# A fused attention and gated feed-forward kernel: the first tokens loaded in four tiles, all weights on one queue, the first ratios sent through DRAM

## Chip, cores and metric

The kernel runs on one core of one Trainium2 chip. The time is the device time of one execution in microseconds (us), and the median of several executions is quoted. Before the change it was 271.02 us (three executions, 270.77 to 271.33). Executions are sorted by state; only fast ones are compared.

Engines in the profile: PE is TensorE (matmul), PEld its weight loads, DVE VectorE, ACT ScalarE, POOL GpSimd, SP SyncE. A row such as `SPq` or `ACTq` is the issue of a transfer by that engine. The row of a stretch has its length, then busy time of PE, PEld, DVE, ACT, POOL, clock, DMA share, GB/s.

## The reference, cut to what matters

```python
# x: 2048 tokens x 512, bf16; 32 heads of 16; 4 segments of 512 tokens; feed-forward 1792 wide
def _A_ref(x, wq, wk, wv, wo, beta):          # attention within a segment, plus a memory of earlier ones
    g = _sigmoid(beta).reshape(1, H, 1, 1)
    for s in range(N):
        logits = q_s @ k_s^T * scale + causal mask
        a_dot = softmax(logits) @ v_s
        a_mem = (phi(q_s) @ M) / (phi(q_s) @ z + 1e-06)      # the "recall"
        o = g * a_mem + (1.0 - g) * a_dot
        M, z = M + phi(k_s)^T @ v_s, z + sum(phi(k_s))
    return o @ wo
def _B_ref(x, W_gate, W_up, W_down):
    return ((x @ W_gate) * relu-mask * (x @ W_up)) @ W_down
g = _sigmoid((x * gate_w).sum(-1, keepdims=True))            # one gate for each token
return g * _A_ref(...) + (1 - g) * _B_ref(...)
```

(The products are abridged; the shapes and the order are the reference's.)

## The kernel before

The kernel gives each instruction as a task with a cost and a priority to a small planner; the planner's simulation fixes the order on each engine, and a table of small shifts (`SHIFT`) tunes that order. Three parts matter here.

The loads at the start. Two engines issue transfers, SyncE (`nc.sync`) and ScalarE (`nc.scalar`):

```python
    def load_halves(dst, src, k, name):
        src = src.rearrange("(c p) n -> p c n", p=P)
        nc.sync.dma_start(out=dst[:, 0:k // 2], in_=src[:, 0:k // 2])
        nc.scalar.dma_start(out=dst[:, k // 2:k], in_=src[:, k // 2:k])
        return [arrival(name + h) for h in "ab"]
    # ...
    got_n[0] = load_halves(xn, x[0:L, :], 4, "n")        # the first 512 tokens, two halves
    got_q = load_halves(wq_sb, A_wq, NC, "q")
    got_k = load_cols(nc.sync, wk_sb, A_wk, 0, D, "k")
    got_v = load_cols(nc.scalar, wv_sb, A_wv, 0, D, "v")
    nc.scalar.dma_start(out=betab[:], in_=A_beta.partition_broadcast(P))   # 64 bytes to each partition
    load_gu(0)
```

The start of TensorE: seven junk matmuls, sixteen transposes of the loaded tokens, then the first projection with wq:

```python
        for k in range(7):
            nc.tensor.matmul(bank(warm[k % 8]), lhsT=junk[:, 0:P], rhs=junk[:], start=True,
                             stop=True)
    # ...
        pairs = [(c, t) for h in range(2) for c in range(2) for t in (2 * h, 2 * h + 1)]
        pairs += [(c, t) for c in (2, 3) for t in range(4)]      # chunk c, token tile t
```

The ratios of the token gates. `rcol` holds them by token; the attention needs them spread over partitions. In the first segment a small matmul spreads them, later ones go through DRAM:

```python
        if seg == 0:
            # ... q0 = rcol * quad on VectorE
            d = plan.add("PE", 260, key, lambda: nc.tensor.matmul(
                bank(sl)[:, 0:16], lhsT=fold.rearrange("p j q -> p (j q)"),
                rhs=q0.rearrange("p b t -> p (b t)"), start=True, stop=True), [d], PEL, need=[sl])
        else:
            a = plan.add("SP", 360, key, lambda: nc.sync.dma_start(
                out=ratio[seg].rearrange("q b t -> b q t"), in_=rcol[:, seg, 0:4]), [c], 2800)
            d = plan.add("SP", 360, key, lambda: nc.sync.dma_start(
                out=rq[seg % 2][:], in_=ratio[seg].rearrange("q b t -> q (b t)")[None]
                .to_broadcast([4, 32, 16])), [a, att.get(("gate", seg - 2))], 2300)
```

The scaled gates `grc` are then one VectorE product, and every attention output of the segment needs them. The recalls of later segments need coefficients `cdr`, which go out to DRAM and come back by two further transfers.

The softmax here doesn't subtract the row's maximum and nothing guards it: scores larger than these inputs give would overflow.

Of the kernel before, what the change touches and what calls it, by code (L numbers as in the profile page):

```python
# [12 lines left out]
P = 128  # L13
# [19 lines left out]
    34: 106376, 36: 113032, 40: -114448, 53: 61670, 57: 13693, 68: 19011, 76: -24569, 79: 9811,  # L33
    83: 74173, 96: 13617, 110: 46210, 203: 58110, 206: -52557, 224: -57564, 227: 1792,
    230: -40586, 233: 13336, 239: 4861, 242: 18866, 245: 1040, 248: -5909, 251: 9703, 254: 598,
    257: 3431, 263: 6249, 265: 184723, 266: 16148, 269: 14619, 272: 3105, 275: 1832, 281: 4406,
    284: 3910, 287: 8594, 289: 93691, 290: -97554, 302: -129776, 339: 46969, 340: 26203,
    351: -125117, 352: -49927, 357: -75265, 365: 12721, 369: 106054, 370: -69909, 374: -148035,
    376: -85788, 378: 3424, 382: 76139, 383: -116528, 389: 34360, 391: 49594, 395: 81165,
    396: 6755, 398: -114708, 404: 5060, 407: -180212, 410: -53419, 413: -3953, 426: 67665,  # L40
    486: 79762, 487: 34701, 549: 20214, 552: 20622, 558: -10377, 561: -19405, 564: 39907,
    570: -12896, 573: 9701, 576: -9651, 582: -16069, 585: 22538, 588: 33613, 591: -4380,
    594: -4590, 603: 3888, 606: 7821, 609: 4156, 612: 8910, 615: -8330, 618: 8398, 624: 10060,
    630: 14623, 633: 38130, 657: -107064, 669: 31434, 682: 109150, 684: -73474, 685: -119916,
    688: 38815, 703: 145579, 705: -95722, 708: 12868, 713: 6919, 726: 31160, 730: 132280,
    734: -54441, 739: -10455, 747: -49618, 752: 229700, 753: -104580, 755: -97169, 761: -147428,
    821: 62605, 851: 29329, 862: -95255, 892: 8128, 895: 66022, 898: 3515, 901: 3081, 904: 8787,
    910: -7899, 913: -6480, 916: -5672, 922: -5022, 928: -20540, 931: -12044, 934: 2538,
    937: 18155, 939: 121046, 940: -2598, 943: 4141, 949: 20268, 955: 16548, 958: -12595,
    964: -16200, 966: -94268, 967: 6793, 973: 22963, 976: 20987, 988: 376830, 1039: 13799,  # L50
    1044: 2818, 1049: -146392, 1054: -57834, 1059: 9401, 1069: -10731, 1071: 101628,
    1074: -107652, 1082: -19522, 1085: 14735, 1088: 14474, 1099: 70503, 1101: 119386,
    1132: -110039, 1161: -106277, 1162: 240923, 1192: -69003, 1212: 109678, 1213: 112279,
    1221: 8139, 1224: 31863, 1227: 14005, 1230: 100895, 1233: 19137, 1236: 79863, 1239: -20537,
    1242: -16128, 1245: -20639, 1248: 150158, 1251: -735, 1254: 26992, 1260: 49993, 1263: 17068,
    1269: 7685, 1272: -7301, 1278: 76110, 1281: 68111, 1284: 44327, 1287: -37198, 1290: 24997,
    1296: -21740, 1299: -12793, 1302: 89596, 1305: -52927, 1329: 147560, 1341: -68166,
    1353: 29837,
# [157 lines left out]
def kernel(  # L216
# [73 lines left out]
    def work():  # L290
# [3 lines left out]
    LANDS = dict(na=4300, nb=4600, qa=5650, qb=6050, k=9300, v=9750, g0=11800, u0=13300, gw=13900, g1=15200, u1=16700,  # L294
                 x1=18400, g2=20400, u2=21600, g3=22800, u3=24000, d0=27700, d1=30400, o=31800, x2=33600)

    def arrival(name):
        return plan.add("in_" + name, 0.0, 0.0, None, lat=LANDS[name])
# [7 lines left out]

    def load_halves(dst, src, k, name):
        src = src.rearrange("(c p) n -> p c n", p=P)
        nc.sync.dma_start(out=dst[:, 0:k // 2], in_=src[:, 0:k // 2])
        nc.scalar.dma_start(out=dst[:, k // 2:k], in_=src[:, k // 2:k])  # L310
        return [arrival(name + h) for h in "ab"]
# [19 lines left out]
    got_n[0] = load_halves(xn, x[0:L, :], 4, "n")  # L331
    got_q = load_halves(wq_sb, A_wq, NC, "q")
    got_k = load_cols(nc.sync, wk_sb, A_wk, 0, D, "k")
    got_v = load_cols(nc.scalar, wv_sb, A_wv, 0, D, "v")
# [6 lines left out]
    got_x[1] = [arrival("x1")] * NC  # L341
    junk = sb([P, L], BF16, "junk")
    nc.vector.memset(junk[:], 0.0)
# [5 lines left out]
    got_x[2] = [arrival("x2")] * NC  # L349
# [20 lines left out]
    for i in range(2):  # L370
        nc.gpsimd.memset(Vp[i][:, :, :, DH:18], 1.0)
        nc.gpsimd.memset(zbd[i][:], 0.0)

    fold = sb([P, 4, 32], F32, "fold")
    nc.vector.tensor_reduce(out=fold[:, 0], in_=ident.rearrange("p (b q) -> p q b", b=4),
                            op=ALU.add, axis=mybir.AxisListType.X)
    nc.vector.tensor_copy(fold[:, 1:4], fold[:, 0:1].to_broadcast([P, 3, 32]))
    quad = sb([P, 4], F32, "quad")
    nc.vector.memset(quad[:], 0.0)
    for b in range(4):  # L380
        nc.vector.memset(quad[32 * b:32 * b + 32, b:b + 1], 1.0)
# [44 lines left out]
    def gate_tasks(seg):  # L426
# [17 lines left out]

        if seg == 0:
            sl, q0 = work(), sb([P, 4, 4], F32, "q0")
            d = plan.add("DVE", 90, key, lambda: nc.vector.tensor_tensor(
                q0[:], rcol[:, seg, None, 0:4].to_broadcast([P, 4, 4]),
                quad[:, :, None].to_broadcast([P, 4, 4]), ALU.mult), [c], DVL, lock=True)
            d = plan.add("PE", 260, key, lambda: nc.tensor.matmul(  # L450
# [457 lines left out]
```

## Time and profile before

| | before |
|---|---|
| median (range), 6 executions beside the changed kernel | 271.17 us (270.70 to 271.76) |
| span of the profiled execution | 270.2 us |
| TensorE busy | 265.3 us, 98% |
| first transpose, first wq matmul | 4.29, 5.97 us |
| first score group | 12.58 us |

A score group is one set of query times key matmuls whose results ScalarE exponentiates in a single 1.88 us instruction. There are 80.

The prediction shows most lines. Two more views are needed. First the DMA rates in the first 12 us, in 40 slices of 0.3 us:

```profile
GB/s 0 0 0 0 0 0 27 79 290 352 375 372 383 382 382 382 379 318 276 348 372 324 307 331 365 379 365 365 379 333 216 122 76 119 208 316 389 386 382 386
```

The rate stays above 270 from 2.4 to 9.0 us. It falls to 76 at about 9.6 us; those are the slices in which beta's small packets run, behind wv on ScalarE's queue. By then wq and wk are in place. Second, the stretch in which the second segment's recalls begin (length, then busy time of PE, PEld, DVE, ACT, POOL, clock, DMA share, GB/s):

```profile
78.00:104.00 26.00, 26.00 (x226) 10.46 (x225) 19.69 (x45) 19.33 (x16) 9.84 (x16) 1.00 0.16 47
```

TensorE is busy in all 26.00 of 26.00 us.

### The profile page before, as it was taken

The numbers are of one execution on the slowest core, as the hardware profiler recorded it, in microseconds if no ns is written. First come the engines' busy times: TensorE is split into PE (matmuls) and PEld (weight loads), VectorE is DVE, ScalarE is ACT, GpSimd is POOL, SyncE is SP. The second block draws the span as 40 slices with busy tenths as digits, with TensorE's granted clock in tenths as the row PEclk, the third lists the DMA queues.
The fourth block names the chain that finished last, engine by engine and source line by source line (L and its number), as shares of the span: only waits on it lengthen the run. The fifth ranks groups of instructions, "written<-read, shape, count | busy, mean of one in ns | idle before, by whom it ended". The sixth has DMA issues, their size and how long they took to land.

```text
span 270.2 us, 5601 instructions
## 1 busy us (share of the span) xinstructions
PE 265.3 (98%) x2247; PEld 112.2 (42%) x2247; DVE 194.8 (72%) x423; ACT 195.5 (72%) x175; POOL 83.6 (31%) x142
## 2 busy tenths in 40 slices
PE   8999999999999999999999999999999999999995
PEld 4443434444443443444443434344344334444543
DVE  4788999999889667999986776689773736285223
ACT  2299899989897768899877896789888678413100
POOL 3013343333343333333324333243333342300000
PEclk9999999999999999999999999999999999999999
DMA  7999991313431103201210021001100120000002
GB/s 231 316 267 347 242 157 21 97 19 79 105 97 31 32 21 120 22 0 22 85 42 22 1 77 35 19 2 58 29 2 0 33 97 22 19 0 2 0 10 68
DMA packets 29841, 19.25 MB, mean 71 GB/s; under 512 B 14840, under 2 KB 28280, under 8 KB 29816
## 3 DMA queue, kind: packets, MB, share of 16 engines
q1 hardware_dynamic: 28600, 17.84, 25.3%
q10 hardware_dynamic: 1216, 1.06, 1.2%
q8 instruction: 17, 0.28, 0.5%
q14 instruction: 8, 0.07, 0.1%
HBM read 13.21 MB, written 2.55 MB: 58 GB/s over the span
## 4 chain that ended last, share of the span: by engine, by line
PE 90%; DMA 3%; DVE 2%; ACT 2%; issue 1%; POOL 0%; SPq 0%; DVEq 0%; ACTq 0%
PE ps L485 71%; PE ps L606 9%; PE ps L648 6%; DMA cdr<-coefs 2%; ACT E L626 2%; PE ps L841 1%; DMA coefs<-dnr 1%; PE ps L735 1%; PE ps L502 1%; PE ps L754 1%; DVE hT L805 0%; POOL E L635 0%; DVE T L680 0%; DVE dnr L719 0%; DVE omr L740 0%
## 5 line engine op out<-in xcount | busy, mean ns | idle before, releaser
L626 ACT ACTIVATE E<-ps 128x2048 bf16<-128x2048 f32 x80 | 150.4, 1880 | 32.0 <-PE ps L606 23.3
L635 POOL TENSOR_SCALAR_AFFINE_SELECT E<-E 128x512 bf16<-128x512 bf16 x128 | 81.4, 654 | 150.4 <-ACT E L626 150.4
L485 PE MATMUL ps<-xT,wg_sb 128*128 128x512 bf16 x224 | 57.8, 380 | 0.0
L485 PE MATMUL ps<-xT,wu_sb 128*128 128x512 bf16 x224 | 56.7, 380 | 0.5 <-DVE omr L740 0.5
L805 DVE TENSOR_TENSOR hT<-ps,rgr 128x512 bf16<-128x512 f32 x56 | 37.7, 685 | 25.7 <-ACT rgr L799 13.6
L485 PE MATMUL ps<-wd_sb,hT 128*128 128x512 bf16 (+1 forms) x238 | 54.9, 367 | 0.0
L799 ACT ACTIVATE rgr<-ps 128x512 bf16<-128x512 f32 x56 | 32.6, 599 | 20.1 <-PE ps L485 19.8
L485 PEld LDWEIGHTS <-hT 128*128 128x128 bf16 x238 | 22.0, 98 | 25.2 <-issue 3.7
L485 PEld LDWEIGHTS <-wu_sb 128*128 128x128 bf16 x224 | 20.4, 98 | 26.5 <-issue 5.0
L485 PEld LDWEIGHTS <-wg_sb 128*128 128x128 bf16 x224 | 20.3, 98 | 25.9 <-issue 4.1
L827 DVE TENSOR_SCALAR osr<-ps,ngcol 128x512 bf16<-128x512 f32 (+1 forms) x17 | 12.0, 708 | 16.9 <-PE ps L485 16.8
L680 DVE STREAM_TRANSPOSE T<-ps 128x512 f32<-128x512 f32 x32 | 20.8, 685 | 3.1 <-PE ps L648 3.0
L648 PE MATMUL ps<-E,Vp 128*17 128x256 bf16 (+3 forms) x512 | 21.3, 300 | 0.0
L485 PE MATMUL ps<-xT,wk_sb 128*128 128x512 bf16 x64 | 17.4, 379 | 0.0
L606 PE MATMUL ps<-QT,KTe 32*128 32x512 bf16 (+3 forms) x256 | 17.3, 302 | 0.0
L606 PE MATMUL ps<-QT,KTo 32*128 32x512 bf16 (+3 forms) x256 | 17.1, 299 | 0.1
L485 PE MATMUL ps<-xT,wq_sb 128*128 128x512 bf16 x64 | 17.1, 389 | 0.0
L485 PE MATMUL ps<-wo_sb,oT 128*128 128x512 bf16 (+1 forms) x68 | 17.0, 367 | 0.0
L485 PE MATMUL ps<-wv_sb,xT 128*128 128x512 bf16 x64 | 16.8, 380 | 0.0
L648 PEld LDWEIGHTS <-Vp 128*17 128x17 bf16 x512 | 10.9, 91 | 12.4 <-issue 3.8
L606 PEld LDWEIGHTS <-KTe 32*128 32x128 bf16 x256 | 5.1, 91 | 20.3 <-issue 19.9
L740 DVE TENSOR_TENSOR omr<-ps,cdr 128x512 bf16<-128x512 f32 x12 | 8.1, 686 | 7.3 <-DMA cdr<-coefs 6.9
(80 smaller groups left out, 207.9 us busy)
## 6 DMA issues: line engine op xcount, KB each, us to landing
cdr<-coefs SPq DMA_DIRECT2D x12, 256.0 KB
out_dram<-osr SPq DMA_DIRECT2D x15, 128.0 KB
wd_sb<-in_B_W_down_dram SPq DMA_DIRECT2D x2, 896.0 KB
xn<-in_A_x_dram SPq DMA_DIRECT2D x3, 512.0 KB
wg_sb<-in_B_W_gate_dram SPq DMA_DIRECT2D x2, 512.0 KB
wu_sb<-in_B_W_up_dram SPq DMA_DIRECT2D x2, 512.0 KB
wg_sb<-in_B_W_gate_dram SPq DMA_DIRECT2D x2, 384.0 KB
wu_sb<-in_B_W_up_dram SPq DMA_DIRECT2D x2, 384.0 KB
```

The costliest lines, as they stand in the source:

```text
L485: nc.tensor.matmul(bank(sl)[:, 0:width], lhsT=lhsT, rhs=rhs, start=(start and q == 0), stop=(stop and q == n - 1))
L502: nc.tensor.transpose(bank(sl[c]).bitcast(BF16)[:, t * P:(t + 1) * P], xn[:, t, c * P:(c + 1) * P], ident[:])
L606: nc.tensor.matmul(ps[:, j * L + off:j * L + off + n], lhsT=kt[32 * j:32 * j + 32, kb * P:(kb + 1) * P], rhs=QT[i][32 * j:32 * j + 32, kb ...
L626: nc.scalar.activation(Ef[:, e0 * L:e1 * L], ps[:, e0 * L:e1 * L], ACT.Exp, scale=SCALE),
L635: nc.gpsimd.affine_select(out=m, in_=m, compare_op=ALU.is_ge, fill=0.0, base=0, pattern=[[0, 4], [1, P]], channel_multiplier=-1)
L648: nc.tensor.matmul(bank(sl)[32 * j:32 * j + HW, kb * P:kb * P + w], lhsT=Vp[i][:, kb, 8 * c + 2 * j + r, 0:HW], rhs=E[(NFILL * u + f) % RE ...
L680: done.append(plan.add("DVE", 633, key - RL, lambda r=r, sl=sl: nc.vector.transpose(T[ts.i][:, r], bank(sl)), [a] + done, 75 if r else 0, ...
L735: a = plan.add("PE", 216, key, lambda: nc.tensor.matmul(bank(sl), lhsT=mbd[i][:, c].rearrange("p j r e -> p (j r e)"), rhs=pqT[u % RQ][:], ...
L740: a = plan.add("DVE", 605, key - RL, lambda: nc.vector.tensor_tensor(omr[om.i][:], bank(sl), cdr[cs.i][:], ALU.mult), [a, b], DVL, need=[o ...
L799: r = plan.add("ACT", 478, key - RL, lambda sl=gsl, rs=rs: nc.scalar.activation(rgr[rs.i][:], bank(sl), ACT.Relu), [g], ACL, frees=[gsl])
L805: nc.vector.tensor_tensor(hT[hs1.i][:], bank(sl), rgr[rs.i][:], ALU.mult)),
L827: b = plan.add("DVE", 95 + 1.12 * w, key - RL, lambda: nc.vector.tensor_scalar(osr[os.i][:, 0:w], bank(sl)[:, 0:w], ngcol[:, tt:tt + 1], N ...
```

## The change

The intent is a shorter start and a little less TensorE work: x arrives in four tiles on two queues and each is transposed when it lands; all weights follow in order on one queue; one warm-up matmul fewer; the ratio matmul goes. The order of everything was fitted again.

```diff
 SHIFT = {                                     # a wholly new table; cut
-    got_n[0] = load_halves(xn, x[0:L, :], 4, "n")
-    got_q = load_halves(wq_sb, A_wq, NC, "q")
+    got_n[0] = [load(nc.scalar if t % 2 else nc.sync, xn[:, t, :], x[t * P:(t + 1) * P, :],
+                     "n%d" % t) for t in range(4)]
+    got_q = [load_cols(nc.sync, wq_sb, A_wq, 256 * i, 256 * i + 256, "q" + "ab"[i])
+             for i in range(2)]
     got_k = load_cols(nc.sync, wk_sb, A_wk, 0, D, "k")
-    got_v = load_cols(nc.scalar, wv_sb, A_wv, 0, D, "v")
+    got_v = load_cols(nc.sync, wv_sb, A_wv, 0, D, "v")
     nc.scalar.dma_start(out=betab[:], in_=A_beta.partition_broadcast(P))
 # cut
-    nc.vector.memset(junk[:], 0.0)
+    nc.vector.memset(junk[:, 0:P], 0.0)
 # cut: fold and quad, the constants of the ratio matmul, go
-        if seg == 0:
-            # cut: the ratio matmul
+        eng, que, cost = ("SP", nc.sync, 360) if seg else ("ACT", nc.scalar, 520)
+        a = plan.add(eng, cost, key, lambda: que.dma_start(
+            out=ratio[seg].rearrange("q b t -> b q t"), in_=rcol[:, seg, 0:4]), [c], 2800)
+        d = plan.add(eng, cost, key, lambda: que.dma_start(
+            out=rq[seg % 2][:], in_=ratio[seg].rearrange("q b t -> q (b t)")[None]
+            .to_broadcast([4, 32, 16])), [a, att.get(("gate", seg - 2))], 2300)
 # cut: transposes and copies of x by token tile, in five parts, the last tile's in two
+        parts = [(0, 0, 4), (1, 0, 4), (2, 0, 4), (3, 0, 2), (3, 2, 4)]
-        for k in range(7):
-            nc.tensor.matmul(bank(warm[k % 8]), lhsT=junk[:, 0:P], rhs=junk[:], start=True,
+        for k in range(6):
+            nc.tensor.matmul(bank(warm[k % 8]), lhsT=junk[:, 0:P],
+                             rhs=junk[:, None, 0:P].to_broadcast([P, 4, P]), start=True,
                              stop=True)
```

## The prediction

> **What bounds the kernel now.** I read the page's header first, then busy time by stretch, then the start of the kernel in order of time, then the waits, and last the two places that those views pointed at.
>
> From the page:
>
> ```profile
> PE 265.3 (98%) x2247; PEld 112.2 (42%) x2247; DVE 194.8 (72%) x423; ACT 195.5 (72%) x175; POOL 83.6 (31%) x142
> PE 90%; DMA 3%; DVE 2%; ACT 2%; issue 1%; POOL 0%; SPq 0%; DVEq 0%; ACTq 0%
> ```
>
> TensorE is the bound: 98% busy, and 90% of the chain that ended last. Busy is not full speed, so I checked the spacing of starts. In this piece, ten full matmuls take from 29.91 to 32.16, 2.25 us: ten times 0.216 and about 0.1 for going from full-array matmuls to the four-row-group ones of L606.
>
> ```profile
> 29.91 1.02 PE L485 MATMUL ps<-xT,wk_sb 128*128 128x512 bf16 x4
> 30.77 1.46 PE L485 MATMUL ps<-xT,wg_sb 128*128 128x512 bf16 x6
> 32.16 0.40 PE L606 MATMUL ps<-QT,KTe 32*128 32x384 bf16 x8
> ...
> 22.42 0.29 PE L450 MATMUL ps<-q,fold 128*128 128x16 f32 x2
> 22.56 0.59 PE L485 MATMUL ps<-xT,wu_sb 128*128 128x512 bf16 x2
> ```
>
> So in the steady part TensorE has nothing to gain except work taken away. The last two lines show one such piece: the first segment's ratio matmul takes 22.42 to 22.56, 0.14 us.
>
> The start, where the change acts:
>
> ```profile
> 0.80 0.46 SPq L309 DMA_DIRECT2D xn<-in_A_x_dram  x1
> 1.25 3.17 PE L841 MATMUL ps<-junk 128*128 128x512 bf16 x7 [1.25 <-DVE mcol_e L359]
> 4.29 1.62 PEld L502 LDWEIGHTS <-xn 128*128 128x128 bf16 x16 [0.78 <-DMA xn<-in_A_x_dram]
> 4.29 1.89 PE L502 MATMUL ps<-ident,xn 128*128 128x128 bf16 x16
> 5.15 0.43 DVE L519 COPY xT<-ps 128x512 bf16<-128x512 bf16 x1 [2.37 <-PE ps L502]
> 5.97 4.08 PE L485 MATMUL ps<-xT,wq_sb 128*128 128x512 bf16 x16
> 6.83 2.73 PEld L485 LDWEIGHTS <-wq_sb 128*128 128x128 bf16 x13 [0.28 <-issue]
> ```
>
> Seven warm-up matmuls (0.43 us each) fill 1.25 to about 4.24; x lands at 4.29; sixteen transposes at 0.105 us run without a gap to 5.97, where the first projection begins. Its first matmuls are still 0.43 us apart (5.97, 6.40, 6.83); the sixteen together end at 9.89, so thirteen take 3.06 and the fast rate begins just after 6.83.
>
> Waits of TensorE and of VectorE on a transfer:
>
> ```profile
> DVE omr L740 <- DMA cdr<-coefs: 6.9, 4, 4.1
> PE ps L485 <- DVE omr L740: 0.5, 1, 0.5
> ...
> 191.14 1.03 PE L485 MATMUL ps<-wv_sb,xT 128*128 128x512 bf16 x4
> 192.62 0.59 PE L485 MATMUL ps<-xT,wu_sb 128*128 128x512 bf16 x2 [0.45 <-DVE omr L740]
> ```
>
> The only real stall after the start is this one: four matmuls from 191.14 should end at 192.00, and the next starts at 192.62, so 0.62 us are lost. Two PSUM banks were held by the memory read-out (recall) while its coefficients came back through DRAM.
>
> **What the Trainium skill says.** "TensorE: Matmul & The Clock Gate", What's actually happening: the clock starts at half speed and is released after a busy window of about 3.4 us; the window is free-running, so the moment varies. The trace agrees in size: starts 0.43 apart until 6.83, then 0.216, so release came 5.6 us after the first warm-up matmul, between one and two windows. Same page, Back-to-back issue gap: N/2.4 + 2.5 ns, 216 ns for 512 columns; the trace has 0.216. "DMA: Bandwidth & Descriptors", Issuing engines are not separate DMA queues: a second issuing engine saves only issue time, which here is 0.46 us a transfer. "Trainium Kernel Development and Optimization", Performance Expectations, says that matmul busy time is a bad measure of the distance to the roofline; the 0.62 us stall below 98% busy agrees, and it is why I count starts and not the 98%.
>
> **The change part by part.**
>
> 1. *Warm-up.* Six matmuls for seven, on a tile whose memset is a quarter as wide (64 columns of 32 bits against 256, 0.27 us now). I take 0.16 off the memset: start at 1.09. Six at 0.43, the first a little shorter as now, end at about 3.63.
>
> 2. *x in four tiles.* Now two 256 KB halves, issued at 0.80 on two queues, the first landing at 4.29. A tile is half of that; at the 335 to 347 GB/s that the busy stretches of the start move, 128 KB less on a shared stream is about 0.4 us earlier on one queue, and 0.7 at best. So the first tile is there at about 3.5 to 3.9, and about when the warm-up ends. I take the transposes to begin at 3.7. Four tiles of four transposes at 0.107 end at 5.41 if each tile lands in time; at 0.43 us a tile against about 0.3 to 0.4 between landings they should.
>
> 3. *The copies move to the end.* This part costs. Before, a chunk of xT over all tokens was copied while the other chunks were transposed, so TensorE went straight on at 5.97. Now every first-projection matmul needs all four tiles, the last too. Its first half is transposed by 5.20, its copy starts about 0.35 us after the start of that last transpose (as now: 4.80 to 5.15), takes about 0.25 (half of 0.43, and a fixed part), and TensorE may go on at about 5.74. So 0.33 us idle, and a first projection at 5.74 instead of 5.97: 0.23 gained.
>
> 4. *Half-speed refund.* If the clock is released at the same moment, the 0.23 us are spent on matmuls at 0.43, worth 0.216 each later: only 0.12 of it stays. Gain 0.12.
>
> 5. *Weights on one queue.* wq comes as two column halves, then wk, then wv. The order of bytes is nearly unchanged; wk now precedes wv where they shared the engines before. The twelve first wq matmuls last until about 9.0, then wk, then wv from 10.7; now both are used by 10.75 with no wait. Hidden: 0.
>
> 6. *First ratios through DRAM.* The TensorE matmul goes: 0.14 gained. The small VectorE set-up (fold, quad) lies in the idle start: 0. In exchange ScalarE issues two transfers, about 0.5 us each as on that queue at the start. The same pair in the second segment, on the other queue, has 2.84 us from the first issue (71.08) to the second (73.92), so with the landing of the second some 5.5 us in all, longer if ScalarE is in the middle of its work. The new order puts the first use of the scaled gates one place before the first use in the normalisation, about 6 us of VectorE work after the transposes that precede it, so it is nearly but not safely hidden.
>
> 7. *New order of everything else.* The shift table is new, so the program's order was fitted afresh. Counting the changes between full, row-group and column-group matmuls in both orders: 177 before, 179 after; at about 0.1 us each that costs 0.2. The work is otherwise the same (2244 matmuls for 2246, the warm-up and the ratio). The recall that stalled now has its second matmul 12 us of TensorE work after its denominators instead of 10, so that only one bank waits: 0.6 gained. Other recalls come closer: one pair at 9.4 to 9.6 us instead of 10.1. The tail has the same last step, a half tile of 256 columns, one VectorE pass and one store.
>
> Sum: -0.12 - 0.14 + 0.2 - 0.6 = -0.66. A new order brings some new wait; I put 0.2 for it, which gives about -0.5: 270.5 us.
>
> **Rivals.**
>
> *A. ScalarE is the bound in the first segment.*
>
> ```profile
> 13.00:50.00 37.00, 37.00 (x284) 14.90 (x284) 33.83 (x84) 34.90 (x37) 12.77 (x20) 1.00 0.84 193
> ```
>
> From 13 to 50 us ScalarE (fourth number, 34.90 of 37.00) has 2.1 us free, and each next score group waits for an exponential. Two issues of 0.5 us may push these back, or VectorE (33.83) may stand at the gates for up to 1 us. For it: little slack. Against: TensorE is saturated there with other work to put between. It would make 271.3 to 271.7.
>
> *B. The clock decides.* The release falls anywhere within a window of some 3.4 us. A second more or less of half speed costs half of itself, and a gap of 0.33 us in front of the projection might even delay the release by a window, 1.7 us of loss. For it: the window is known to be free-running, and the three runs before differ by 0.56. Against: the present start already is a mixture of warm-up and transposes and was released. It would make 269.5 if early, 272 if late.
>
> *C. The front gain is whole.* If the release follows the start, and the copies are quicker than I take them, 0.5 us are gained in front: 270.0.
>
> *D. Nothing but the stall.* The start gains zero because the first weights or the last tile are late; then 270.8.
>
> **Range and chances.** The middle is 270.5. A and the late release of B lie above, C and an early release below, each about 1 us, and single medians move by 0.3: 269.5 to 271.6. A change of 2% would be 5.4 us, ten times the sum of all terms, and no rival reaches it: 0.98 for within 2%, 0.01 on either side.
>
> **What would show it.** Step 1: first warm-up matmul at about 1.1. Step 2: first transpose at about 3.7. Step 3: a TensorE gap of about 0.3 us and a first wq matmul at about 5.7, with xT copies in front of it as the releaser. Step 4: starts 0.43 apart until about 6.8. Step 6: no matmul of the ratio, and no VectorE wait on rq. Step 7: no wait at the recall near 190 us, TensorE still about 98% busy. I am wrong if a wait on ScalarE or on rq shows in the first 50 us, if wk or wq delays the projection, or if a bank stall of over 0.6 us stands elsewhere.

## The result, and the profile after

| | before | after |
|---|---|---|
| median (range), 6 executions each | 271.17 (270.70 to 271.76) | 278.77 (278.01 to 279.68) |
| ratio, 95% interval | | 1.028 (1.0253 to 1.0307): slower |
| span of the profiled execution | 270.2 | 277.3 |
| first transpose, first wq matmul | 4.29, 5.97 | 3.61, 7.34 |
| starts of score groups 1, 9, 11 | 12.58, 35.18, 40.37 | 14.83, 38.30, 46.04 |
| starts of score groups 23, 31, 80 | 73.11, 95.05, 231.08 | 79.31, 103.71, 236.72 |

A ratio here is the mean time of one kernel's fast runs over that of the other's fast runs of the same rounds, so it is not quite the ratio of the medians. All these runs were fast, at a granted clock of 0.994 to 1.0.

The page, engines and chain of the last work:

```profile
PE 263.2 (95%) x2209; PEld 112.4 (41%) x2244; DVE 187.9 (68%) x415; ACT 196.4 (71%) x176; POOL 83.7 (30%) x142
...
PE 63%; DMA 15%; DVE 7%; issue 2%; ACT 1%; SPq 1%; DVEq 0%
```

TensorE's share of the chain falls from 90% to 63%, and transfers go from 3% to 15%. (35 matmul records are missing, 2209 against 2244 weight loads, and the few "issue" gaps of TensorE are those.) The waits of TensorE:

```profile
PE ps L464 <- DVE hT L783: 2.2, 1, 2.2
...
PE ps L464 <- DMA wq_sb<-in_A_wq_dram: 1.8, 1, 1.8
PE ps L626 <- DVE omr L718: 1.1, 3, 0.6
...
PE ps L713 <- DVE T L658: 0.4, 1, 0.4
PE ps L464 <- DVE osr L805: 0.4, 1, 0.4
```

The large ones lie in three places.

**The start**, in order of time:

```profile
1.05 2.74 PE L819 MATMUL ps<-junk 128*128 128x512 bf16 x6 [1.05 <-DVE mcol_e L358]
...
1.73 0.97 SPq L304 DMA_DIRECT2D wq_sb<-in_A_wq_dram  x2
1.73 0.45 ACTq L334 DMA_DIRECT2D betab<-in_A_beta_dram  x1
...
3.61 1.90 PE L487 MATMUL ps<-ident,xn 128*128 128x128 bf16 x16
...
5.54 0.37 ACT L493 COPY xT<-ps 128x256 bf16<-128x256 bf16 x1 [0.27 <-PE ps L487]
...
7.34 3.89 PE L464 MATMUL ps<-xT,wq_sb 128*128 128x512 bf16 x11 [1.84 <-DMA wq_sb<-in_A_wq_dram]
...
9.88 0.15 PEld L464 LDWEIGHTS <-wq_sb 128*128 128x128 bf16 x1 [0.28 <-issue]
10.21 0.74 PEld L464 LDWEIGHTS <-wq_sb 128*128 128x128 bf16 x4 [0.18 <-issue]
```

The tokens are ready at 5.91, earlier than before, but wq is not: TensorE idles 1.84 us. Then TensorE is still at about half speed for seven wq matmuls (the last only in part) instead of two: eleven take 3.89 us, and the weight loads, one every 0.43 us up to 9.88, become four in 0.74 from 10.21. The sum fits: the first wq matmul is 7.34 - 5.97 = 1.37 later, the slow ones lose 1.35 us against the rate of 0.216 here and 0.47 before, 0.88 more, and together that is 2.25, by which group 1 is later (14.83 - 12.58).

The wait belongs to the change. The slow matmuls need not follow from it: f2 below has the same loads at the start and waits as long, and in its profile no wq matmul was slow:

```profile
7.29 2.76 PE L470 MATMUL ps<-xT,wq_sb 128*128 128x512 bf16 x12 [1.79 <-DMA wq_sb<-in_A_wq_dram]
```

The DMA rates in slices of 0.3 us show why wq is late:

```profile
GB/s 0 0 0 0 0 0 147 195 232 335 352 324 249 209 127 106 83 54 87 116 204 301 282 332 360 374 362 382 386 382 372 345 355 355 341 352 345 355 345 341
```

From 4.2 to 6.0 us the rate is at most 127 and down to 54 GB/s, where before it was 276 to 382. In just that time the packets of ScalarE's queue are beta's, of 64 bytes; they run from 3.7 to 7.0 us. wq's first half lands at 7.32 us.

**The first gates:**

```profile
30.93 1.12 ACTq L436 DMA_DIRECT2D ratio<-rcol  x1
...
35.70 0.57 ACTq L438 DMA_DIRECT2D rq<-ratio  x1
...
42.49 0.37 DVE L451 TENSOR_TENSOR grc<-rq,gcat 128x128 f32<-128x128 f32 x1 [2.53 <-DMA rq<-ratio]
...
45.09 1.02 PE L464 MATMUL ps<-xT,wg_sb 128*128 128x512 bf16 x4 [2.21 <-DVE hT L783]
```

The trip takes 42.49 - 30.93 = 11.56 us. VectorE stands still for 2.53 us, and TensorE, which needs VectorE's next result, for 2.21. From group 9 to group 11, with the same order on TensorE, the time is 7.74 us here; f2 and f4 below, which send nothing through DRAM here, have 5.19.

**The second segment's recalls:**

```profile
83.26 0.61 SPq L710 DMA_DIRECT2D cdr<-coefs  x1
...
84.53 0.58 SPq L710 DMA_DIRECT2D cdr<-coefs  x1
...
90.02 0.69 DVE L718 TENSOR_TENSOR omr<-ps,cdr 128x512 bf16<-128x512 f32 x1 [2.52 <-DMA cdr<-coefs]
...
90.76 0.72 PE L626 MATMUL ps<-E,Vp 128*17 128x512 bf16 x16 [0.65 <-DVE omr L718]
```

Two transfers bring coefficients of two groups of heads. The group recalled first uses the second one, which lands at 89.93; its bank stays occupied, and TensorE waits. The stretches in figures:

```profile
13.00:50.00 37.00, 34.03 (x255) 13.81 (x259) 29.84 (x78) 31.27 (x34) 10.79 (x17) 1.00 0.96 202
78.00:104.00 26.00, 23.62 (x174) 9.54 (x175) 20.18 (x51) 19.63 (x17) 8.46 (x14) 1.00 0.25 58
```

TensorE's 37.00 and 26.00 of before are 34.03 and 23.62 now (missing records included). The DMA engines are at 0.96 in the first stretch and at 0.25 in the second: the first segment's ratios travel while the weights of the feed-forward still come in.

To split the difference I counted, for each kernel's own order, when each score group would start if all matmuls ran at the steady rate (0.216 us for 512 columns, 0.1 for each change of array mode) and took the excess of the measured start. It is an estimate from the trace's durations. Excess in us:

| score group | 1 | 11 | 23 | 31 | 65 | 67 | 80 |
|---|---|---|---|---|---|---|---|
| before | 4.0 | 4.1 | 3.9 | 3.8 | 3.6 | 4.2 | 4.1 |
| after | 6.5 | 9.1 | 9.4 | 11.7 | 11.5 | 11.5 | 11.7 |
| difference | 2.5 | 5.1 | 5.5 | 7.9 | 7.9 | 7.2 | 7.5 |

So 2.5 us are lost in front (the 2.25 from above, and 0.22 for the warm-up matmul that was taken away without any gain), 2.5 at the gates, some 2.5 from group 23 to 31, and 0.6 come back where before had its stall near 192 us.

### The profile page after: what moved, and what is told of

Read it like the earlier page. It is cut to its first block, busy times and chain, and to the rows that moved or that the text cites. A ratio compares the mean times of both kernels' runs of the same rounds, so it can differ in the third digit from the quotient of the medians.

```text
span 277.3 us, 5578 instructions
## 1 busy us (share of the span) xinstructions
PE 263.2 (95%) x2209; PEld 112.4 (41%) x2244; DVE 187.9 (68%) x415; ACT 196.4 (71%) x176; POOL 83.7 (30%) x142
## 4 chain that ended last, share of the span: by engine, by line
PE 63%; DMA 15%; DVE 7%; issue 2%; ACT 1%; SPq 1%; DVEq 0%
PE ps L464 50%; PE ps L584 6%; DMA cdr<-coefs 6%; PE ps L626 6%; DMA coefs<-dnr 3%; DMA rq<-ratio 2%; DVE T L658 2%; DMA ratio<-rcol 2%; DMA out_dram<-osr 1%; DVE dnr L697 1%; DVE omr L718 1%; DVE osr L805 1%; SPq L710 1%; ACT E L604 1%; PE ps L713 1%
## 5 line engine op out<-in xcount | busy, mean ns | idle before, releaser
L464 PE MATMUL ps<-xT,wg_sb 128*128 128x512 bf16 x219 | 56.9, 380 | 2.7 <-DVE hT L783 2.2
L464 PE MATMUL ps<-xT,wu_sb 128*128 128x512 bf16 x216 | 55.4, 380 | 0.6 <-issue 0.3
L464 PE MATMUL ps<-wd_sb,hT 128*128 128x512 bf16 (+1 forms) x230 | 53.0, 366 | 1.2 <-issue 0.6
L464 PE MATMUL ps<-wo_sb,oT 128*128 128x512 bf16 (+1 forms) x65 | 16.3, 366 | 0.5 <-issue 0.5
L522 DVE CAST QT<-ps 128x512 bf16<-128x512 f32 x16 | 10.8, 676 | 5.2 <-PE ps L464 5.1
```

The lines of the kernel that those rows point to most:

```text
L464: nc.tensor.matmul(bank(sl)[:, 0:width], lhsT=lhsT, rhs=rhs, start=(start and q == 0), stop=(stop and q == n - 1))
L522: prj["q", seg, c] = plan.add("DVE", 600, key - RQK, lambda: nc.vector.tensor_copy(QT[i][:], bank(sl)), [a], DVL, frees=[sl])
```

## The experiments

Eighteen kernels ran, in batches on one chip each, always beside the kernel before, whose median was 271.12 to 271.54. The theory: three separate costs. BETA: beta's small packets, moved forward, slow the weights behind them. GATE: the trip of the first ratios. ORDER: the second segment's coefficients in the wrong order. Rivals were the column halves of wq (512-byte pieces), the half-speed clock, the engine that issues the trip, and the number of x transfers. Where I say nothing, the result was correct.

### First batch: which part costs

**e1_beta_late**: the changed kernel, beta's transfer moved behind the later load of gate_w.

```diff
-    nc.scalar.dma_start(out=betab[:], in_=A_beta.partition_broadcast(P))
     load_gu(0)
     nc.sync.dma_start(out=gwb[:], in_=gate_w.partition_broadcast(P))
     got_gw = arrival("gw")
+    nc.sync.dma_start(out=betab[:], in_=A_beta.partition_broadcast(P))
```

> The changed kernel with one transfer moved: the 8 KB broadcast of beta goes out on the weight queue behind gate_w instead of right behind x on the second queue. Orders on all engines are otherwise the same. Theory BETA (the broadcast's 64-byte packets slow the shared engines while wq comes in; traced from 4.0 to 7.0 us): first half of wq there by about 5.5, first wq matmul at 5.6 to 5.9 instead of 7.34, time 276.3 to 277.0. Rival COLUMNS (wq in column halves means 512-byte packets, and those are slow): first wq matmul stays after 7, time stays 278.0 to 279.5.

Measured: 278.42 us (275.24 to 278.97), ratio 1.0237. The first wq matmul came at 6.71, still after a wait of 1.6 us, and group 1 at 12.86 in place of 14.83. The front gains 2 us in the profile, which is of the fastest execution: 0.63 by the earlier weights, the rest because no wq matmul ran at half speed here. The median hardly moves, because the spread has grown to 3.7 us. Beta is not all, and one profile does not speak for such a median.

**e2_wq_rows**: wq in halves of rows (1 KB pieces), beta as changed.

```diff
-    got_q = [load_cols(nc.sync, wq_sb, A_wq, 256 * i, 256 * i + 256, "q" + "ab"[i])
+    got_q = [load(nc.sync, wq_sb[:, 2 * i:2 * i + 2],
+                  A_wq.rearrange("(c p) n -> p c n", p=P)[:, 2 * i:2 * i + 2], "q" + "ab"[i])
              for i in range(2)]
```

> The changed kernel with wq in two row halves (1 KB packets) instead of two column halves; beta stays right behind x. Theory COLUMNS: first wq matmul at 5.6 to 5.9, time about 276.5. Theory BETA: packets of 1 KB take a somewhat larger share beside the 64-byte ones, but the first wq matmul stays after 6.5 and the time gains less than 1 us.

Measured: 277.42 (276.70 to 280.57), ratio 1.0263; first wq matmul at 7.67. Whole rows do not bring the weights earlier. The small pieces are not the cause.

**e3_gate_free**: the first gates are computed from a tile of ones; both transfers still run. The result is wrong (relative error 0.030).

```diff
+    rfix = sb([P, 4, 4], F32, "rfix")
+    nc.gpsimd.memset(rfix[:], 1.0)
-            rq[seg % 2].rearrange("p b t -> p t b")[:, None].to_broadcast([P, 8, 4, 4]),
+            (rq[seg % 2] if seg else rfix).rearrange("p b t -> p t b")[:, None].to_broadcast([P, 8, 4, 4]),
```

> The changed kernel with a wrong result on purpose: the gates of the first segment read a tile of ones set at the start, so nobody waits for the ratios' way through DRAM; both transfers still run. Theory GATE (VectorE stands 2.5 us before the gates and TensorE with it for 2.2): no VectorE wait there, time lower by 2.0 to 2.5, 276.3 to 276.8. Rival: VectorE or TensorE meets another wait right after, time lower by less than 1 us.

Measured: 276.78 (275.79 to 278.27), ratio 1.0205: 2.0 us less than the changed kernel. Groups 9 to 11 take 5.37 us, against 7.74. VectorE's wait was real; taking it away gives most of the 2.5 us. The weight lies on the times, for this wait differs between executions: e1, which still reads the ratios from DRAM, took 5.41 us in its profile, with 0.4 us of waiting.

**e4_beta_late_gate_free**: the diffs of e1 and e3 together (wrong).

> Both edits at once (wrong result on purpose). What is left of the loss is then the stretch from 78 to 100 us, where the changed kernel fell back by another 2.4 us. Theory FOLLOW-ON (those waits come because everything before was late against transfers): they vanish and the time is 270.3 to 271.5. Rival OWN ORDER (the new order of instructions has these waits by itself): time 273.3 to 274.3.

Measured: 277.55 (276.03 to 278.68), ratio 1.0226. The two gains did not add up. First wq matmul at 5.88, but from group 1 to group 9 there are 27.14 us (23.47 in the changed kernel), with TensorE 4.0 us in wait of exponentials. ScalarE in order of time:

```profile
30.42 1.12 ACTq L438 DMA_DIRECT2D ratio<-rcol  x1
...
31.59 1.88 ACT L606 ACTIVATE E<-ps 128x2048 bf16<-128x2048 f32 x1 [1.37 <-PE ps L586]
...
37.67 0.56 ACTq L440 DMA_DIRECT2D rq<-ratio  x1
...
38.34 1.88 ACT L606 ACTIVATE E<-ps 128x2048 bf16<-128x2048 f32 x1 [3.86 <-DMA ratio<-rcol]
```

The second transfer reads what the first wrote, so ScalarE has to stand until the first has landed, 7.25 us after its issue, with the next exponentials behind it. The trip can hold up even a kernel that never reads its result: a second way in which GATE costs, which I had not seen before.

### Second batch: mending the parts

**f1_front_gate**: beta late, wq in row halves, and the ratios spread by sixteen small GpSimd copies in place of the two transfers.

```diff
+        def spread_first():
+            for b in range(4):
+                for k in range(4):
+                    nc.gpsimd.tensor_copy(rq[0][32 * k:32 * k + 32, b, :],
+                                          rcol[32 * b:32 * b + 32, 0, 0:4])
         # segment 0: emitted where the first transfer was issued; the second issue goes
```

> The changed kernel with beta behind gate_w, wq in row halves, and the first segment's ratios spread by sixteen 32x4 copies on GpSimd instead of two transfers from ScalarE's queue (correct result). Theory SCALARE QUEUE (the second transfer waits in ScalarE's stream for the first one's landing, holding back exponentials, so taking only VectorE's wait away gained little): no loss between 30 and 46 us; first wq matmul by 6.0; left is the stretch from 78 to 100 us with 1.4 to 2.6 us: 272.0 to 273.8, and the runs lie within 1 us of each other. Rival: another wait takes its place and the time stays above 275.

Measured: 274.51 (273.39 to 275.45), ratio 1.0114. First wq matmul at 5.91, group 1 at 12.04.

**f2_gate_pool**: only the GpSimd copies, that is the diff of f1 on the changed kernel, with beta and wq as changed.

> The changed kernel with the GpSimd copies alone; beta and wq as in the changed kernel. Theory SCALARE QUEUE: the whole loss between 30 and 46 us goes, 2.5 to 3.5 us, so 275.0 to 276.3; the front is as late as before (first wq matmul at 6.7 to 7.4). Theory GATE (VectorE's wait alone): no more gained than by e3_gate_free, 276.8.

Measured: 276.11 (275.80 to 278.57), ratio 1.0202. Groups 9 to 11 take 5.19 us and no wait on a gate is left; the first wq matmul stays at 7.29. GATE in full is worth 278.77 - 276.11 = 2.7 us, and the front (beta and row halves) 276.11 - 274.51 = 1.6.

**f3_cols_gate**: f1 with wq in column halves again.

```diff
-    got_q = [load(nc.sync, wq_sb[:, 2 * i:2 * i + 2],
-                  A_wq.rearrange("(c p) n -> p c n", p=P)[:, 2 * i:2 * i + 2], "q" + "ab"[i])
+    got_q = [load_cols(nc.sync, wq_sb, A_wq, 256 * i, 256 * i + 256, "q" + "ab"[i])
              for i in range(2)]
```

> As f1_front_gate but with wq in column halves. In e1 the weights were slow from 3.5 to 5.2 us though no beta was under way, in e4 they were not. Theory COLUMNS: 0.3 to 1.5 us slower than f1_front_gate on average, first wq matmul between 5.9 and 6.8, and a wider spread of the times. Theory BETA ALONE: the same as f1_front_gate within 0.3 us.

Measured: 273.63 (272.98 to 276.14), ratio 1.0101; first wq matmul at 5.43. No slower than f1. With e2 this ends the rival of the small pieces. f3 differs from f2 by beta's place alone, so it also gives the cleanest measure of BETA in the changed kernel: 276.11 - 273.63 = 2.5 us. That, too, rests on the times (four executions each): in the profiles f3 leads f2 by 1.24 us at group 1, but only by 0.12 at group 11.

**f4_front_gate_swap**: f1, and in the second segment the coefficients of the heads recalled first are sent first.

```diff
         # cut: each transfer is kept as fetches[seg, c]
+        other = {(1, 0): (1, 1), (1, 1): (1, 0)}.get((seg, c), (seg, c))
+        b = plan.add("SP", 360, key - 3000, lambda: fetches[other](),
```

> As f1_front_gate, and in the second segment the coefficients of the head group that is recalled first are sent first (in the changed kernel they are sent second, 1.27 us later). Theory OWN ORDER (the recall holds a bank until its coefficients land, and the matmuls on E need that bank): the wait of TensorE at the first recall shrinks by about 1 us, time 0.8 to 1.3 below f1_front_gate: 271 to 272.7. Rival: the next waits (transposes of T, output tiles) are late by themselves and take it back, less than 0.4 us gained.

Measured: 273.02 (272.18 to 273.31), ratio 1.0056 (1.0036 to 1.0075), 1.5 us under f1. The read-out now waits for TensorE's recall and not for the transfer:

```profile
85.08 0.69 DVE L730 TENSOR_TENSOR omr<-ps,cdr 128x512 bf16<-128x512 f32 x1 [1.14 <-PE ps L725]
...
85.84 1.26 PE L633 MATMUL ps<-E,Vp 128*17 128x512 bf16 x32
```

Groups 23 to 31 take 22.30 us; in f1 they take 23.74, in the changed kernel 24.40. ORDER is confirmed: swapping two issues, with all engines' compute order unchanged, gives the 1.5 us. In every fast profile of the changed kernel's order without the swap this stretch takes 23.45 to 24.92 us, in the four with it (f4, h0, h1, m4) 21.95 to 22.96. One loss at the start is left: the first wq matmul comes at 5.89, but the third, which needs wq's second half, only at 7.21.

### Third batch: the converse

**e5_before_beta_early**: the kernel before, with beta's transfer directly behind x on ScalarE's queue. One line moves, nothing else.

```diff
     got_n[0] = load_halves(xn, x[0:L, :], 4, "n")
+    nc.scalar.dma_start(out=betab[:], in_=A_beta.partition_broadcast(P))
     got_q = load_halves(wq_sb, A_wq, NC, "q")
     got_k = load_cols(nc.sync, wk_sb, A_wk, 0, D, "k")
     got_v = load_cols(nc.scalar, wv_sb, A_wv, 0, D, "v")
-    nc.scalar.dma_start(out=betab[:], in_=A_beta.partition_broadcast(P))
```

> The kernel before with one transfer moved: beta's broadcast directly behind its half of x on the second queue, so ahead of that queue's half of wq, as it is placed in the changed kernel. Theory BETA: the weights slow down while it runs, the first wq matmul comes 1 to 2 us later than 5.97, time 271.8 to 273.2. Rival (what slows the changed kernel's front is its single weight queue or the column halves): first wq matmul stays near 6.0, time within 0.4 us of before.

Measured: 275.48 (275.29 to 275.84), ratio 1.0161 (1.0139 to 1.0183): 4.3 us lost to 8 KB. The wait, and the DMA rates in slices of 0.3 us:

```profile
PE ps L485 <- DMA wq_sb<-in_A_wq_dram: 2.7, 1, 2.7
```

```profile
GB/s 0 0 0 0 0 0 106 130 259 348 328 362 372 295 112 22 50 50 126 149 150 190 218 275 315 355 369 379 386 386 382 382 386 362 345 345 348 348 348 348
```

The rate drops to 22 GB/s from 4.5 us on. The first wq matmul starts at 8.64; after two at full speed seven run at half speed, and group 1 begins at 16.58 instead of 12.58; no later loss follows. BETA is shown, and bigger than I had expected, perhaps because here wq's second half stands on ScalarE's own queue behind beta too (not tested apart).

**h0_front_swap_scalar_gate** and **h1_front_swap_sync_gate**: f4 with the trip of the ratios put back, issued by ScalarE (h0) or by SyncE (h1).

```diff
         # abridged: in place of f4's spread_first on GpSimd, the two transfers of the change
+        eng, que, cost = ("SP", nc.sync, 360) if seg else ("ACT", nc.scalar, 520)   # h0
+        eng, que, cost = ("SP", nc.sync, 360) if seg else ("ACT", nc.sync, 520)     # h1
```

> f4_front_gate_swap with the first ratios back on their way through DRAM from ScalarE's queue: only the gates differ between the two. Theory SCALARE QUEUE: 2 to 5 us slower than f4_front_gate_swap, 275.0 to 278.0, with ScalarE's exponential held by the landing of the ratios and VectorE by rq. Rival (the gate loss was a follow-on of the late front): within 1 us of f4_front_gate_swap.

> As h0, but the two transfers are issued from the sync queue at the same place of the order. Theory SCALARE QUEUE: no exponential waits for a landing any more; what is left is VectorE's wait for rq, and the time lies between f4 and h0: 273.5 to 275.5. Rival (the trip itself, not the engine that issues it): as slow as h0.

Measured: h0 275.71 (274.22 to 277.82), ratio 1.0174; h1 275.61 (274.39 to 277.97), ratio 1.0175. Both 2.6 to 2.7 us above f4, the same as f2's gain from the other side. In h0 TensorE waits 2.3 us for exponentials; in h1 ScalarE is free of the issues, and TensorE waits 1.8 us for VectorE's copy of Vp next to the late gates. Moving the issue to another engine did not bring the time down; the trip is the cost. (The issues did not stand at the same time: SyncE, busy with other transfers, sent the first one at 33.17 us in h1, ScalarE at 29.26 in h0. Yet the second, which waits for its landing, followed at 35.28 and 35.27.)

**k1_before_tiles**: the kernel before with x in four tiles on two queues, transposed tile by tile, and six warm-ups on the small tile; beta, wq and the ratio matmul as before.

```diff
-    got_n[0] = load_halves(xn, x[0:L, :], 4, "n")
+    for t in range(4):
+        (nc.scalar if t % 2 else nc.sync).dma_start(out=xn[:, t, :], in_=x[t * P:(t + 1) * P, :])
 # cut: the arrivals, transposes by token tile, copies in five parts, six warm-ups as in the change
```

> The part of the change that can pay, alone in the kernel before: x in four tiles on two queues, transposed tile by tile, six warm-up matmuls on the small tile; weights, beta, gates and the order of all else as before. First wq matmul at 5.4 to 5.8 instead of 5.97. Theory FRONT: 0.1 to 0.5 us faster than before, 270.6 to 271.1. Rival: the gap before the first projection and the half-speed clock take it back, within 0.1 us or slower.

Measured: 273.25 (272.34 to 274.58), ratio 1.0078 (1.0032 to 1.0123). The change's own start is 2.0 us slower than the old one even with beta out of the way:

```profile
PE ps L487 <- DMA wq_sb<-in_A_wq_dram: 1.6, 1, 1.6
```

```profile
GB/s 0 0 0 0 0 0 41 215 348 372 348 348 154 89 201 208 239 311 341 362 369 376 358 389 369 379 375 365 339 307 286 250 171 147 168 263 329 386 376 365
```

The first transpose begins at 3.59, the first wq matmul at 7.07, and seven run at half speed: 1.10 us of delay and 1.02 more lost by slow matmuls than before make 2.12, and group 1 is 2.11 later (14.69). The rate dips to 89 GB/s at about 4 us, with no packets of beta under way.

### Fourth and fifth batch: the start

k1 was a surprise, so six more runs went into it.

**m1_before_x_four**: the kernel before, only x in four transfers. **m2_before_tiles_x_two**: k1 with x in two halves again. **m3_before_warm6**: the kernel before with only the six warm-ups. **m4_swap_x_two**: f4 with x in two halves.

```diff
 # m1, against before (m2 takes the same back from k1)
-    got_n[0] = load_halves(xn, x[0:L, :], 4, "n")
+    for t in range(4):
+        (nc.scalar if t % 2 else nc.sync).dma_start(out=xn[:, t, :], in_=x[t * P:(t + 1) * P, :])
 # cut: the arrivals
 # m3, against before
-    nc.vector.memset(junk[:], 0.0)
+    nc.vector.memset(junk[:, 0:P], 0.0)
-        for k in range(7):
-            nc.tensor.matmul(bank(warm[k % 8]), lhsT=junk[:, 0:P], rhs=junk[:], start=True,
+        for k in range(6):
+            nc.tensor.matmul(bank(warm[k % 8]), lhsT=junk[:, 0:P],
+                             rhs=junk[:, None, 0:P].to_broadcast([P, 4, P]), start=True,
 # cut: the rest of the call
 # m4, against f4 (the arrivals cut)
-    got_n[0] = [load(nc.scalar if t % 2 else nc.sync, xn[:, t, :], x[t * P:(t + 1) * P, :],
-                     "n%d" % t) for t in range(4)]
+    for h, eng in enumerate((nc.sync, nc.scalar)):
+        eng.dma_start(out=xn[:, 2 * h:2 * h + 2],
+                      in_=x[256 * h:256 * h + 256, :].rearrange("(c p) n -> p c n", p=P))
```

> The kernel before with one thing changed: x comes in four tiles, two on each queue, in place of two halves; the order on TensorE and VectorE is the same row by row. FOUR (four transfers ahead of the weights delay the weights by themselves): the first wq matmul at 6.8 to 7.2 us as in the full-tile version instead of 5.97, the wait named wq, and 272.5 to 273.5 us. RIVAL, EARLY TRANSPOSES (TensorE being ready sooner, and the copies at the end, only expose weights that are no later than before): the first wq matmul at 5.9 to 6.1 and 271 us.

> The full-tile version of the kernel before (273.25 us, first wq matmul 7.07) with x loaded in two halves again; tile-wise transposes and copies, and the six warm-ups on the small tile, stay. FOUR: the weights land at about 5.6 and 6.05 us again, the first wq matmul at 5.9 to 6.2, and 271 to 271.6 us. RIVAL, EARLY TRANSPOSES: 6.8 to 7.2 and 273 us again.

> The kernel before with six warm-up matmuls on the small tile in place of seven on the whole one; nothing else. Warm-up from about 1.05 to 3.6, then a gap of about 0.6 to the first transpose at 4.29, because x lands no sooner. If the clock takes a gap badly (rival B of the prediction), up to five more matmuls 0.43 apart and up to 1 us more, 272 us; otherwise 271.0 to 271.4, no more than 0.2 us from the kernel before.

> The best mended version so far (273.02 us; first wq matmul 5.89) with x in two halves in place of four tiles. FOUR: weights at least as early, and less spread between executions; first wq matmul 5.7 to 6.0 and 272.2 to 273.0 us. RIVAL (with beta out of the way the number of x transfers doesn't matter): 273.0 within 0.4 us. In neither case is the kernel before (271.2) beaten by 2%.

Measured: m1 271.75, its four fast executions between 271.14 and 271.88, ratio 1.0019 (1.0005 to 1.0033). Its profile fell in a slow execution (338.01 us, granted clock 0.756), so its trace is not compared, and the expected start of wq could not be checked. m2 271.22 (270.68 to 272.21), ratio 1.0007; first wq matmul at 6.06 after 0.58 us of waiting for the copies. m3 271.21 (271.14 to 271.68), ratio 1.0008; first wq matmul at 5.65. m4 272.69 (271.59 to 274.12), ratio 1.0064, within the spread of f4.

So the tile-wise transposes cost nothing when x comes in two transfers, nor does the shorter warm-up. The four transfers cost 0.5 us alone (m1), and 2.0 where the transposes go by tile too (k1 against m2), so that TensorE is ready earlier and then idle. In neither form does this start beat the old one.

**n1_tiles_filled** and **n2_after_filled**: k1 and the changed kernel with seven junk matmuls in front of the first wq matmul, so that TensorE doesn't idle there.

```diff
+                for _ in range(7):
+                    nc.tensor.matmul(bank(sl), lhsT=junk[:, 0:P],
+                                     rhs=junk[:, None, 0:P].to_broadcast([P, 4, P]), start=True,
+                                     stop=True)
```

> The full-tile version of the kernel before (273.25 us; first wq matmul 7.07; 1.6 us of idle TensorE, then six matmuls at half speed) with seven more junk matmuls between the transposes and the first wq matmul, so that TensorE is not idle while it waits for the weights; every other row of the order is the same. CLOCK (most of the 2 us is the clock that the gap keeps or puts at half speed): no wq matmul, or at most two, 0.43 us apart, although the weights still land at about 7 us, and 1.0 to 1.4 us less, 271.9 to 272.3. RIVAL, WEIGHTS (the late landing itself): the wq matmuls at full speed but 273 us within 0.4.

> The changed kernel (278.77 us; first wq matmul 7.34; seven wq matmuls 0.43 us apart) with the same seven junk matmuls. CLOCK: at most two wq matmuls 0.43 us apart and the first score group about 1.0 to 1.4 us earlier than the changed kernel's, 277.2 to 277.8 us if nothing later takes it back. RIVAL, GATE: the time stays at 278.8 within 0.7, because the wait at the first segment's gates (2.5 us at 38 to 46 us) is set by ScalarE and by two transfers, which get no earlier.

Measured: n1 273.12 (271.93 to 273.64), ratio 1.0056 (1.0032 to 1.0079), with before at 271.54 in that batch. All sixteen wq matmuls ran at full speed, 6.38 to 10.01, and group 1 began at 12.94, but against the kernel before of its batch the median gained only some 0.5 us on k1 (1.58 above it in place of 2.04), with overlapping intervals: by the number the rival (the late landing itself) did better; in the profile 0.7 of the 1.75 us gained at group 1 are lost again by group 9, with a wait of 0.5 us for the next segment's xT. n2 276.34 (275.43 to 278.00), ratio 1.0184: 2.4 us less than the changed kernel, more than either theory had said.

```profile
5.39 1.67 PE L521 MATMUL ps<-junk 128*128 128x512 bf16 x7 [0.27 <-DVE xT L493]
...
8.36 2.76 PE L464 MATMUL ps<-xT,wq_sb 128*128 128x512 bf16 x12 [1.30 <-DMA wq_sb<-in_A_wq_dram]
```

Although the weights came 1 us later in this execution (8.36), twelve matmuls take 2.76 us, none at half speed. For that lateness group 1 gains only 0.3 us. The rest comes at the gates: in this execution the ratios landed in time, and groups 9 to 11 took 5.24 us. Whether that is owed to the filler or to a good execution, one profile can't say.

The two runs do not show that the filler kept the clock up. In both, full speed came before it: the transposes go from 0.107 us apart to 0.056 at about 4.2 us, and the junk matmuls from 4.81 (n1) and 5.39 (n2) are 0.216 apart from the first. And e1, e2, e3 and f2, without filler, waited 1.6 to 2.0 us for wq with no wq matmul at half speed, while h1 waited 0.7 and had eight. Of the six profiles with a wait of 1.6 to 2.0 us only two, the changed kernel's and k1's, had slow wq matmuls. The idle time of TensorE may play a part, but no run here shows it; n2's gain of 2.4 us in the median is clear (the intervals of the ratios, 1.0154 to 1.0215 and 1.0253 to 1.0307, lie apart) and unexplained.

### The main versions of the changed kernel

| run | median | ratio | first wq matmul | groups 9 to 11 | groups 23 to 31 |
|---|---|---|---|---|---|
| changed kernel | 278.77 | 1.028 | 7.34 | 7.74 | 24.40 |
| e1 beta late | 278.42 | 1.0237 | 6.71 | 5.41 | 24.23 |
| e3 gates of ones | 276.78 | 1.0205 | 7.18 | 5.37 | 24.63 |
| f2 GpSimd copies | 276.11 | 1.0202 | 7.29 | 5.19 | 24.92 |
| f1 copies, beta late, rows | 274.51 | 1.0114 | 5.91 | 6.54 | 23.74 |
| f3 copies, beta late, columns | 273.63 | 1.0101 | 5.43 | 6.32 | 24.87 |
| f4: f1 and coefficients swapped | 273.02 | 1.0056 | 5.89 | 5.19 | 22.30 |
| m4 and x in two | 272.69 | 1.0064 | 5.74 | 6.32 | 21.95 |
| before | 271.17 | 1 | 5.97 | 5.19 | 21.94 |

(The last row's order on TensorE is another one, so its group intervals only give a scale. In f1 and m4 the longer way from 9 to 11 goes with a wait of TensorE of 0.8 us on VectorE's Vp and of 0.7 on its hT.) No version beats the kernel before. What remains of m4, 1.5 us, was not tested; its profile shows waits of 0.7 us each on VectorE's hT and QT, which the new order brings.

## Why the prediction was wrong

The prediction said 270.5 us and 0.98 for "within 2%"; the result was 278.77 and slower. Its account of the bound was right: TensorE, with nothing to gain but work or stalls taken away. That is just why new waits counted. (A small slip in its reading: from 6.83 to 9.89 fourteen matmuls run, not thirteen, for the weight loads counted there run one ahead.)

- **Steps 1 and 2 were right.** First warm-up matmul at 1.05 (1.09 predicted), transposes from 3.61 (3.7).
- **Step 3 holds only where the weights come early.** It put the first wq matmul at 5.74. With beta late it was 5.43 to 6.19 in seven kernels (e4, f1, f3, f4, h0, h1, m4) and 6.71 in e1; in the changed kernel it was 7.34. Even then later matmuls could wait for the rest of wq, as in f4 (the third at 7.21).
- **Step 4**, a gain of 0.12 from the clock, assumed a release at the same moment as before. In the profiled execution the slow wq matmuls lost 0.88 us more instead, but not because of the gap of 1.84 us alone: e1, e2, e3 and f2 had such gaps and no slow wq matmul. Rival B's first half fits best, that the release falls anywhere: full speed came at about 4.2 us in n2 and 10.2 in the changed kernel. How often the other executions of the changed kernel lost it is not on record, so that part may be bad luck.
- **Step 5 is the step that failed first**: "The order of bytes is nearly unchanged", "Hidden: 0". The bytes were, the neighbours were not. Beta's 8 KB moved from behind wv to directly behind x, and the rate fell to 54 GB/s while wq was in flight. e5 shows it on the old kernel, 4.3 us, and f3 against f2 on the changed one, 2.5. A second cost at the start, the four transfers of x, was taken as a pure gain in step 2; m1 shows 0.5 us and k1 2.0. In the profiles the front cost 2.5 us, the slow clock's 0.88 included, in place of a gain of 0.1.
- **Step 6 was mis-sized**: the trip was put at 5.5 us and "nearly but not safely hidden". It took 11.56 us; from ScalarE's first issue to the second landing it was 8.4 us at the least, in n2. The 2.84 us taken from the second segment was measured where the DMA engines had little to do; here they were at 0.96. Rival A had the right mechanism, VectorE standing at the gates and ScalarE's issues, at up to 1 us; f2, h0 and h1 give 2.6 to 2.7. It saw the 0.5 us of each issue, not the wait for the landing between them.
- **Step 7 was half right.** Two more changes of array mode, and the old stall of 0.6 us is gone. But "I put 0.2" for a new wait was 2.5 us: the second segment's recalls, whose coefficients come in the wrong order. f4's swap gives 1.5 of it back. It could have been read from the order of issues against the order of recalls, which I did not compare.

The three failures measured separately, 1.6 (front, f1 against f2; f3 gives 2.5), 2.7 (gates, f2) and 1.5 (order, f4 against f1), sum to 5.8 of the 7.6 us, or 6.7 with f3.

What stays open: what sets the moment of full speed at the start, and why four transfers of x delay what follows them. k1's dip at 4 us has no small packets to blame, it was weaker in n1 with the same transfers, and m4 with two had one from 4.5 to 6.3 us. The runs show that it varies between executions, not its cause.

## What to carry to other kernels

Moving a transfer to another queue moves everything behind it forward: look at what then stands next to the first weights, even if it is 8 KB and its line is not in the diff. A trip through DRAM has to be sized where it will run, at the DMA load of that moment, and if its second half reads its first, the issuing engine stands in between; sixteen small copies on an idle engine were cheaper. And where transfers and their users are ordered by two separate rules, compare the two orders.

## What the Trainium skill lacked or had wrong

- "DMA: Bandwidth & Descriptors", Queues, rings and completion order, says that the engines take turns between queues packet by packet. It does not say what a small broadcast beside bulk loads costs: 8 KB in 64-byte packets took the rate from over 350 to 22 GB/s and the kernel 4.3 us (e5).
- The same page, Anatomy of one DMA, gives about 2 us of fixed cost. Here the two small transfers of the ratios took 4.77 us (30.93 to 35.70, the second issue) and 6.8 us (to 42.49) with the DMA engines at 0.96 of busy time. The page has that measure for another issue path, and says that load raises the latency; a size for a whole small transfer at such a load is missing.
- No page says that four transfers in place of two can delay those behind them: 0.5 us alone (m1), 2.0 with transposes by tile (k1 against m2).
- "TensorE: Matmul & The Clock Gate", What's actually happening, explains by a free-running window that the moment of full speed varies, by 0.5 us either way. Here it varied more: full speed came at about 4.2 us in n2 and 10.2 in the changed kernel, with the same instructions up to 4.9 us and then gaps, and no run shows what decides it. The granted clock of the profile does not show the slow start: it reads 1.00 in the changed kernel's slow stretch (7.3 to 10 us; its page has no PEclk row at all), while it is 0.56 in e5's (8.6 to 12 us). Go by the starts.
- No page fits the slow execution into which this program on one core fell once (m1: 338.01 us, granted clock 0.756); the runs do not show why.
